# Block-sparse attention into a soft mixture of experts: the chunk selection packed two row blocks to a transpose

## The chip, the cores and the metric

One core of one Trainium2 chip runs the whole kernel in one launch. The metric is the device time of that launch in microseconds (us). The three runs before the change took 177.64, 177.72 and 176.17 us; their median is 177.64.

## The reference

Attention with a per-query choice of key chunks comes first: 4 batches, 8 heads, 768 positions, head size 64. Keys are grouped in 24 chunks of 32. For every query an upper bound of its score against each chunk is made from the chunk's elementwise minimum and maximum; the six causal chunks with the highest bound stay, all other keys are masked. A soft mixture of experts over 3072 tokens follows (512 features, 8 experts, 4 slots each).

```python
k_min, k_max = np.min(k_chunks, axis=3), np.max(k_chunks, axis=3)
ub = np.sum(np.maximum(q * k_min, q * k_max), axis=-1)          # per query and chunk
ub = np.where(causal, ub, -1000000000.0)
top_chunks = np.argsort(ub, axis=-1)[..., -top_k:]              # top_k = 6
scores = scale * np.matmul(q, k.transpose(0, 1, 3, 2))
mask = sel & (pos[:, None] >= pos[None, :])
attn = softmax(np.where(mask, scores, -1000000000.0))
x = np.matmul(attn, v)                                          # then tokens x features
logits = x @ phi                                                # (3072, 32)
slot_input = softmax(logits, axis=0).T @ x
slot_out = per_expert(relu(slot_input @ w1) @ w2)
return softmax(logits, axis=1) @ slot_out
```

## The kernel before

Heads are worked in pairs: 16 pairs, one per iteration `i` of the main loop (line 469), with 128 positions as a *row block* (six per pair, `NQT`). The two heads of a pair lie on partitions 0 to 63 and 64 to 127. The instruction order on each engine is written out by hand (`tc.manual_schedule()`), as a software pipeline: iteration `i` computes scores and exponentials of pair `i` (six groups `g`, `scores` and `expo`), the bounds and the selection of pair `i+1` (`ubound`, `select`, `ns_transposes`, `evac_ns`), loads, transposes and chunk minima and maxima of pair `i+2` (`transposes`, `evac_T`, `kmin`, `kmax`, `qsplit`), the product with V of pair `i-1` (`pv`), and the normalised output of pair `i-2`. After every fourth pair a batch is complete, and the `moe_*` steps of that batch (logits, running softmax, dispatch) are put into the iterations that follow: `moe_logits` at the ends of iterations 5, 9 and 13, `moe_max` to `moe_ct` in 6, 10 and 14. After the loop come the last batch, the experts and the output.

Who does what. TensorE (PE) does every product and transpose. ScalarE (ACT) does all exponentials (line 289) and copies the transposed k and q out of PSUM (line 193). VectorE (DVE) does minima and maxima, the top-8 search (line 242), the comparison (line 245), the copy of the transposed selection (line 261), normalisation and the rest of the copies. GpSimd (POOL) issues all input DMAs (lines 120, 127, 132) and masks the diagonal blocks (line 291). Each iteration asks for k and q of pair `i+4`, v of pair `i+2` and, in most iterations, 1 MB of expert weights, all on one DMA queue.

The selection goes through these tiles. `ub_ps` holds the bounds, `[128 queries, 6 row blocks, 2 heads x 24 chunks]`. `mx` takes the eight largest of each 24. `ns_t` (two static buffers) is a row of 64 columns per head and row block: in columns 0 to 23 a 1 where the chunk is *not* selected, in column 24 the largest bound (written by POOL, line 244), zeros beyond. Six PE transposes (line 253) turn it into `ns_ps`, with the heads on partitions 0 to 63 and 64 to 127, and DVE copies 768 columns to `nsT`. In `scores`, each group adds to the products of k and q, in the same PSUM tile, a second product of `smask` and `nsT`: `smask` has -1e9 in the rows of a chunk and -1 in row 24, so unselected keys sink and the largest bound is subtracted before the exponential. A group is up to 512 query columns of one or two key blocks:

```python
GROUPS = [[(0, 0, 512, 0)], [(1, 0, 512, 0)], [(2, 0, 512, 0)],
          [(4, 0, 256, 0), (0, 512, 256, 256)],
          [(3, 0, 384, 0), (1, 512, 128, 384)], [(5, 0, 128, 0)]]
```

The two score buffers (`p_sc`, `bufs=2`) alternate, so group `g+2` cannot start before the exponential of group `g` has read its buffer. The PSUM pool `p_tp` (two buffers) serves all transposes, bounds, logits and small products in turn.

Of the kernel before, what the change touches and what calls it, by code (L numbers as in the profile page):

```python
# [10 lines left out]
F32 = mybir.dt.float32  # L11
BF16 = mybir.dt.bfloat16
ALU = mybir.AluOpType
# [4 lines left out]
NEG = -1e9  # L18
CH = 32
NCHUNK = 24  # L20
NQT = 6
P = 128
S = 768
# [23 lines left out]
def kernel(  # L47
# [10 lines left out]
    nc = tc.nc  # L58
# [12 lines left out]
    static = ctx.enter_context(tc.tile_pool(name="static", bufs=1))  # L71
# [4 lines left out]
    p_tp = ctx.enter_context(tc.tile_pool(name="p_tp", bufs=2, space=PSUM))  # L76
    st = {}
# [7 lines left out]
    c_pad = static.tile([P, NQT, 4, CH], BF16, name="c_pad")  # L85
# [6 lines left out]
    identf = static.tile([P, P], F32, name="identf")  # L92
    ones_sq = static.tile([P, P], BF16, name="ones_sq")
    caus = static.tile([P, NQT, 2, NCHUNK], BF16, name="caus")
    qgrp = static.tile([P, 4, CH], BF16, name="qgrp")
    smask = static.tile([P, NQT, 4, CH], BF16, name="smask")
    schunk = static.tile([P, NCHUNK, 1], BF16, name="schunk")
    headsel = static.tile([P, 1, 2, 1], BF16, name="headsel")
    ns_t = [static.tile([P, NQT, 2, 64], BF16, name=f"ns_t{i}") for i in range(2)]

    small = ctx.enter_context(tc.tile_pool(name="small", bufs=1))
    xp = ctx.enter_context(tc.tile_pool(name="xp", bufs=2))
# [3 lines left out]
    tp2 = i_ctx.enter_context(tc.tile_pool(name="tp2", bufs=2, side="right"))  # L106
# [5 lines left out]
    def load_w(i):  # L112

        if i < E:
            src = moe_w1[i].rearrange("(a p x) f -> p a (x f)", p=P, x=2)
            dst = w_sb[i].rearrange("p (a f) -> p a f", a=NDG // 2)
        else:
            src = moe_w2[i - E].rearrange("(a p x) d -> p a (x d)", p=P, x=4)
            dst = w_sb[i].rearrange("p (a f) -> p a f", a=NFG // 4)
        nc.gpsimd.dma_start(out=dst, in_=src)  # L120

    def load(i, nm):

# [16 lines left out]
    make_identity(nc, ident)  # L140
    load(1, "k")
    load(1, "q")
    for t in (caus, qgrp, headsel, schunk, ns_t[0], ns_t[1], c_pad):
        nc.vector.memset(t, 0.0)
    nc.vector.memset(ones_sq, 1.0)
    for t in v_t:
# [1 line left out]
    for h in range(2):  # L148
# [10 lines left out]
    load(2, "k")  # L159
    load(2, "q")  # L160
    load_w(0)
    for h in range(2):
        sl = schunk[h * 64:(h + 1) * 64]
        nc.gpsimd.affine_select(
            out=sl, in_=sl, compare_op=ALU.not_equal, fill=NEG, base=0,
            pattern=[[-1, NCHUNK], [0, 1]], channel_multiplier=1,
        )
        nc.gpsimd.affine_select(
            out=sl, in_=sl, compare_op=ALU.not_equal, fill=-1.0, base=-NCHUNK,
            pattern=[[0, NCHUNK], [0, 1]], channel_multiplier=1,  # L170
        )
    load_v(0)
    load_v(1)
    nc.gpsimd.dma_start(out=phi_sb, in_=moe_phi.rearrange("(hg p) s -> p hg s", p=P))
# [45 lines left out]
        st["qpn", i] = t  # L220

    def ubound(i):
        ps = p_tp.tile([P, NQT, 2 * NCHUNK], F32, name="ub_ps", tag="tp")
        qpn, bd = st.pop(("qpn", i)), st.pop(("bd", i))
        for t in range(NQT):
            nc.tensor.matmul(
                ps[:, t, :], lhsT=qgrp.rearrange("p a b -> p (a b)"),
                rhs=caus[:, t].rearrange("p h c -> p (h c)"), start=True, stop=False,
            )
            for x in range(2):  # L230
                nc.tensor.matmul(  # L231
                    ps[:, t, :], lhsT=qpn[:, x, t * P:(t + 1) * P],
                    rhs=bd[:, x].rearrange("p h c -> p (h c)"),
                    start=False, stop=(x == 1),
                )
        st["ubps", i] = ps

    def select(i):
        ub = st.pop(("ubps", i)).rearrange("p t (h c) -> p (t h) c", h=2)
        mx = tpu.tile([P, NQT * 2, 8], F32, name="mx", tag="mx")  # L240
        for a in range(NQT * 2):
            nc.vector.max(mx[:, a, :], ub[:, a, :])  # L242
        ns = ns_t[i % 2].rearrange("p t h c -> p (t h) c")
        nc.gpsimd.tensor_copy(ns[:, :, NCHUNK:NCHUNK + 1], mx[:, :, 0:1])
        nc.vector.tensor_tensor(
            ns[:, :, :NCHUNK], ub,
            mx[:, :, TOPK - 1:TOPK].broadcast_to([P, NQT * 2, NCHUNK]), op=ALU.is_lt,
        )

    def ns_transposes(i):  # L250
        ps = p_tp.tile([P, NQT, P], BF16, name="ns_ps", tag="tp")
        for t in range(NQT):
            nc.tensor.matmul(  # L253
                ps[:, t, :], lhsT=ns_t[i % 2][:, t].rearrange("p h c -> p (h c)"),
                rhs=ident, is_transpose=True,
            )
        st["nsps", i] = ps

    def evac_ns(i):
        t = tp2.tile([P, S], BF16, name="nsT", tag="nsT")  # L260
        nc.vector.tensor_copy(t, st.pop(("nsps", i)).rearrange("p t c -> p (t c)"))  # L261
        st["nsT", i] = t

    def scores(i, g):
        ps = p_sc.tile([P, 2, 512], F32, name="sc_ps", tag="sc")
        kT, qT, nsT = st["kT", i], st["qT", i], st["nsT", i]
        for kg, q0, w, c in GROUPS[g]:
            qs = slice(kg * P + q0, kg * P + q0 + w)
            for h in range(2):
                r = slice(h * 64, (h + 1) * 64)  # L270
                nc.tensor.matmul(  # L271
                    ps[:, h, c:c + w], lhsT=kT[r, kg * P:(kg + 1) * P], rhs=qT[r, qs],
                    start=True, stop=False,
                )
            for h in range(2):
                r = slice(h * 64, (h + 1) * 64)
                nc.tensor.matmul(  # L277
                    ps[:, h, c:c + w], lhsT=smask[r, kg].rearrange("p a b -> p (a b)"),
                    rhs=nsT[r, qs], start=False, stop=True,
                )  # L280
        st["scps", i, g] = ps

    def expo(i, g):
# [185 lines left out]
    for i in range(-2, NPAIR):  # L469
# [64 lines left out]
        if have(i + 2):  # L534
            qsplit(i + 2)
        if i == -2:
            nc.scalar.copy(smask.rearrange("p t a x -> p (t a) x"), schunk.broadcast_to([P, NCHUNK, CH]))
        moe(moe_ct, i - 3)
        moe(moe_logits, i - 2)
        moe(moe_copy, i - 2)  # L540
# [33 lines left out]
    op = ctx.enter_context(tc.tile_pool(name="op", bufs=5))  # L574
# [3 lines left out]
    for g in range(2):  # L578
        sl = slice(g * 16, (g + 1) * 16)
# [5 lines left out]
    for g in range(2):  # L585
        sl = slice(g * 16, (g + 1) * 16)
# [121 lines left out]
```

## Time and profile before

| What | Value |
|---|---|
| Runs | 177.64, 177.72, 176.17 us |
| The profiled execution: its time, its span | 177.53 us, 175.8 us |
| PE busy (share of the span) | 139.1 us (79%) |
| DVE busy | 128.8 us (73%) |
| ACT busy | 120.0 us (68%) |
| POOL busy | 99.9 us (57%) |
| Bytes moved by DMA | 32.92 MB, mean 187 GB/s |

The span runs from the first to the last instruction of the program; 1.7 us of the execution lie around it. A busy share says how long an engine had something in work, not that it sets the pace: the 16 iterations, the first loads and the end after the loop have different limits, and the sections on them must be read one by one. Matmuls are pipelined and their ends are modelled, so a PE that is nearly always busy need not be at its limit. Times in the prediction are counted from the span's start.

### The profile page before, as it was taken

The numbers are of one execution on the slowest core, as the hardware profiler recorded it, in microseconds if no ns is written. First come the engines' busy times: TensorE is split into PE (matmuls) and PEld (weight loads), VectorE is DVE, ScalarE is ACT, GpSimd is POOL, SyncE is SP. The second block draws the span as 40 slices with busy tenths as digits, with TensorE's granted clock in tenths as the row PEclk, the third lists the DMA queues.
The fourth block names the chain that finished last, engine by engine and source line by source line (L and its number), as shares of the span: only waits on it lengthen the run. The fifth ranks groups of instructions, "written<-read, shape, count | busy, mean of one in ns | idle before, by whom it ended". The sixth has DMA issues, their size and how long they took to land.

```text
span 175.8 us, 5994 instructions
## 1 busy us (share of the span) xinstructions
PE 139.1 (79%) x2486; PEld 95.9 (55%) x2486; DVE 128.8 (73%) x429; ACT 120.0 (68%) x163; POOL 99.9 (57%) x194
## 2 busy tenths in 40 slices
PE   0449888999889889999988999999689569986500
PEld 0334556777567657766765776677467444532000
DVE  4456979999889998999998999999752650246530
ACT  2336798989789778988977698897667321156430
POOL 7995679869768557877775585759344600000000
PEclk9999999999999999999999999999999956999755
DMA  3999999999999999999999999199999993009995
GB/s 50 167 158 180 194 206 200 206 197 209 179 212 193 215 185 143 200 172 203 172 147 203 169 207 141 17 187 211 200 214 214 213 215 72 4 13 403 402 405 212
DMA packets 40460, 32.92 MB, mean 187 GB/s; under 512 B 26353, under 2 KB 34545, under 8 KB 40433
## 3 DMA queue, kind: packets, MB, share of 16 engines
q0 software_dynamic: 38416, 26.25, 101.8%
q1 hardware_dynamic: 2016, 6.29, 9.1%
q8 instruction: 19, 0.31, 0.7%
q14 instruction: 9, 0.07, 0.1%
HBM read 52.49 MB, written 6.29 MB: 334 GB/s over the span
## 4 chain that ended last, share of the span: by engine, by line
PE 36%; ACT 19%; DVE 13%; DMA 12%; POOL 11%; issue 5%; POOLq 0%; DVEq 0%; ACTq 0%
ACT e_sb L289 13%; DMA k_in<-in_k_dram 7%; PE sc_ps L271 6%; DMA out_dram<-o_sb 5%; PE at_ps L308 5%; PE sc_ps L277 4%; PE tr_ps L184 3%; PE h_ps L605 3%; DVE x_sb L321 3%; POOL e_sb L291 3%; POOL q_in L127 2%; PE ns_ps L253 2%; POOL k_in L127 2%; PE so_ps L640 2%; PE si_ps L427 2%
## 5 line engine op out<-in xcount | busy, mean ns | idle before, releaser
L289 ACT ACTIVATE e_sb<-sc_ps 128x1024 bf16<-128x1024 f32 x96 | 83.6, 936 | 10.9 <-PE sc_ps L277 9.9
L291 POOL TENSOR_SCALAR_AFFINE_SELECT e_sb<-e_sb 128x256 bf16<-128x256 bf16 x96 | 39.5, 423 | 32.7 <-ACT e_sb L289 32.0
L271 PE MATMUL sc_ps<-qT,kT 64*128 64x512 bf16 (+3 forms) x256 | 39.6, 310 | 6.6 <-ACT e_sb L289 6.3
L277 PE MATMUL sc_ps<-nsT,smask 64*128 64x512 bf16 (+3 forms) x256 | 36.8, 306 | 0.0
L308 PE MATMUL at_ps<-v_t,e_sb 128*128 128x65 bf16 x672 | 29.4, 194 | 1.2 <-DVE x_sb L321 1.1
L308 PEld LDWEIGHTS <-e_sb 128*128 128x128 bf16 x672 | 25.1, 98 | 3.4 <-DVE x_sb L321 1.6
L271 PEld LDWEIGHTS <-kT 64*128 64x128 bf16 x256 | 15.8, 94 | 16.8 <-issue 8.7
L242 DVE MAX8 mx<-ub_ps 128x8 f32<-128x24 f32 x192 | 18.8, 170 | 4.6 <-PE ub_ps L231 4.5
L202 DVE TENSOR_REDUCE mm<-kT 128x24 bf16<-128x768 bf16 x16 | 15.2, 949 | 4.0 <-ACT kT L193 4.0
L132 POOL DMA_DIRECT2D v_t<-in_v_dram x16 | 16.7, 1042 | 1.9 <-PE ns_ps L253 1.2
L193 ACT COPY kT<-tr_ps 128x768 bf16<-128x768 bf16 x16 | 12.8, 803 | 6.5 <-PE tr_ps L184 6.5
L321 DVE TENSOR_TENSOR x_sb<-at_ps,inv 128x768 bf16<-128x768 f32 (+2 forms) x17 | 15.5, 910 | 0.6
L277 PEld LDWEIGHTS <-smask 64*128 64x128 bf16 x256 | 13.1, 95 | 4.4 <-issue 0.3
L208 DVE TENSOR_REDUCE mm<-kT 128x24 bf16<-128x768 bf16 x16 | 15.1, 942 | 0.0
L193 ACT COPY qT<-tr_ps 128x768 bf16<-128x768 bf16 x16 | 13.2, 825 | 2.7 <-PE tr_ps L184 2.7
L184 PE MATMUL tr_ps<-ident,k_in 128*64 128x128 bf16 x192 | 9.2, 237 | 6.6 <-DMA k_in<-in_k_dram 5.5
L670 DVE TENSOR_SCALAR o_sb<-o_ps,cinv 128x512 f32<-128x512 f32 x12 | 8.6, 748 | 7.2 <-PE o_ps L668 4.1
L231 PE MATMUL ub_ps<-bd,qpn 128*128 128x48 bf16 x192 | 10.4, 187 | 2.8 <-DVE qpn L218 2.5
L127 POOL DMA_DIRECT2D k_in<-in_k_dram x16 | 11.7, 729 | 1.3 <-POOLq L692 0.8
L261 DVE COPY nsT<-ns_ps 128x768 bf16<-128x768 bf16 x16 | 8.9, 556 | 4.0 <-PE ns_ps L253 3.5
L672 ACT ACTIVATE o_sb<-o_ps,cinv 128x512 f32<-128x512 f32 x12 | 7.8, 688 | 5.7 <-DMA out_dram<-o_sb 3.8
L127 POOL DMA_DIRECT2D q_in<-in_q_dram x16 | 11.5, 721 | 0.0
(95 smaller groups left out, 213.2 us busy)
## 6 DMA issues: line engine op xcount, KB each, us to landing
w_sb<-in_moe_w_dram POOLq DMA_DIRECT2D x16, 1024.0 KB, 12.9
out_dram<-o_sb SPq DMA_DIRECT2D x10, 512.0 KB, 5.5
k_in<-in_k_dram POOLq DMA_DIRECT2D x16, 192.0 KB, 7.9
q_in<-in_q_dram POOLq DMA_DIRECT2D x16, 192.0 KB, 8.1
v_t<-in_v_dram POOLq DMA_DIRECT2D x16, 192.0 KB, 9.3
out_dram<-o_sb SPq DMA_DIRECT2D x4, 256.0 KB, 3.4
phi_sb<-in_moe_phi_dram POOLq DMA_DIRECT2D x1, 32.0 KB, 9.6
```

The costliest lines, as they stand in the source:

```text
L127: nc.gpsimd.dma_start(out=t, in_=src.rearrange("h (p g) d -> p h (g d)", p=P))
L132: nc.gpsimd.dma_start(out=v_t[i % NV][:, :, :, :D], in_=v[b, 2 * j:2 * j + 2].rearrange("h (g p) d -> p h g d", p=P),)
L193: nc.scalar.copy(t.rearrange("d (p g) -> d p g", g=NQT), st.pop((nm + "ps", i)).rearrange("d g p -> d p g"),)
L202: nc.vector.tensor_reduce(mm[:, 0, 0, :], kT, axis=AX.X, op=ALU.min)
L208: nc.vector.tensor_reduce(mm[:, 1, 0, :], kT, axis=AX.X, op=ALU.max)
L242: nc.vector.max(mx[:, a, :], ub[:, a, :])
L271: nc.tensor.matmul(ps[:, h, c:c + w], lhsT=kT[r, kg * P:(kg + 1) * P], rhs=qT[r, qs], start=True, stop=False,)
L277: nc.tensor.matmul(ps[:, h, c:c + w], lhsT=smask[r, kg].rearrange("p a b -> p (a b)"), rhs=nsT[r, qs], start=False, stop=True,)
L289: nc.scalar.activation(e[:, :, :w], st.pop(("scps", i, g))[:, :, :w], func=ACT.Exp, scale=scale)
L291: nc.gpsimd.affine_select(out=e[:, :, :P], in_=e[:, :, :P], compare_op=ALU.is_ge, fill=0.0, base=0, pattern=[[0, 2], [1, P]], channel_mult ...
L308: nc.tensor.matmul(o, lhsT=st["e", i, g][:, h, c:c + P], rhs=v_t[i % NV][:, h, kg, :], start=(kg == 0), stop=(kg == t),)
L321: nc.vector.tensor_tensor(st["x", b][:, t0:t1, 2 * j:2 * j + 2, :].rearrange("p t h d -> p h t d"), at[:, :, :, :D], inv.broadcast_to([P, ...
```

## The change

The selection row shrinks from 64 to 32 columns per head and row block, and two neighbouring row blocks (`2j` and `2j+1`, the last index `x` of the bounds tile) share one transpose: `ns_t` is `[128, 3, 2 heads, 2, 32]`. Three transposes per pair replace six, and the copy to `nsT` has 384 columns instead of 768. After the transpose a head's 64 partitions hold the even row block in their first 32 rows and the odd one in the other 32, in the same columns. `smask` therefore exists twice, once with its rows filled in the first half of a head's partitions and once in the second; the other half is zero. A mask product over several row blocks becomes two, one for the blocks of the first one's parity and one for the others, each writing every second 128-column block of the PSUM tile (`2*m-1` blocks in steps of two); a single block needs one, as before. Per pair and head this makes 14 mask products out of 8. The top-8 search of row block `t` reads only the first `4t+4` chunks (at least 8) instead of 24. In the setup, two selects over 96 columns replace four over 24, one small DVE addition joins the heads' halves, and the ACT copy that spreads `schunk` to `smask` has 1536 columns instead of 768. Order of work on every engine, and everything not named here, stays.

```diff
-    smask = static.tile([P, NQT, 4, CH], BF16, name="smask")
-    schunk = static.tile([P, NCHUNK, 1], BF16, name="schunk")
+    smask = static.tile([P, 2, NQT, 4, CH], BF16, name="smask")
+    NJ = NQT // 2
+    squad = static.tile([P, 2, 2, NCHUNK], BF16, name="squad")
+    schunk = static.tile([P, 2, NCHUNK, 1], BF16, name="schunk")
...
-    ns_t = [static.tile([P, NQT, 2, 64], BF16, name=f"ns_t{i}") for i in range(2)]
+    ns_t = [static.tile([P, NJ, 2, 2, CH], BF16, name=f"ns_t{i}") for i in range(2)]
...
-    for h in range(2):
-        sl = schunk[h * 64:(h + 1) * 64]
-        nc.gpsimd.affine_select(out=sl, ...)
-        nc.gpsimd.affine_select(out=sl, ...)
+    nc.gpsimd.affine_select(out=squad, ...)
+    nc.gpsimd.affine_select(out=squad, ...)
...
     def ubound(i):
-        ps = p_tp.tile([P, NQT, 2 * NCHUNK], F32, name="ub_ps", tag="tp")
+        ps = p_tp.tile([P, NJ, 2, 2, NCHUNK], F32, name="ub_ps", tag="tp")
         for t in range(NQT):
+            o = ps[:, t // 2, :, t % 2, :]
...
     def select(i):
         for a in range(NQT * 2):
-            nc.vector.max(mx[:, a, :], ub[:, a, :])
+            t = 2 * (a // 4) + a % 2
+            nc.vector.max(mx[:, a, :], ub[:, a, :max(8, 4 * t + 4)])
...
     def ns_transposes(i):
-        for t in range(NQT):
+        for t in range(NJ):
...
     def evac_ns(i):
-        t = tp2.tile([P, S], BF16, name="nsT", tag="nsT")
+        t = tp2.tile([P, NJ * P], BF16, name="nsT", tag="nsT")
...
     def scores(i, g):
-            for h in range(2):
-                r = slice(h * 64, (h + 1) * 64)
-                nc.tensor.matmul(
-                    ps[:, h, c:c + w], lhsT=smask[r, kg].rearrange("p a b -> p (a b)"),
-                    rhs=nsT[r, qs], start=False, stop=True,
-                )
+            t0, n = kg + q0 // P, w // P
+            for x in range(min(2, n)):
+                f = t0 + x
+                m = (n - x + 1) // 2
+                k0 = c // P + f - t0
+                for h in range(2):
+                    r = slice(h * 64, (h + 1) * 64)
+                    nc.tensor.matmul(
+                        ps[:, h].rearrange("p (k y) -> p k y", y=P)[:, k0:k0 + 2 * m - 1:2, :],
+                        lhsT=smask[r, f % 2, kg].rearrange("p a b -> p (a b)"),
+                        rhs=nsT[r, f // 2 * P:(f // 2 + m) * P].rearrange("p (k y) -> p k y", y=P),
+                        start=False, stop=(x == min(2, n) - 1),
+                    )
...
         if i == -2:
-            nc.scalar.copy(smask.rearrange("p t a x -> p (t a) x"), schunk.broadcast_to([P, NCHUNK, CH]))
+            nc.vector.tensor_tensor(schunk[:, :, :, 0], squad[:, :, 0, :], squad[:, :, 1, :], op=ALU.add)
+            nc.scalar.copy(
+                smask.rearrange("p o t a x -> p (o t a) x"),
+                schunk.rearrange("p o c x -> p (o c) x").broadcast_to([P, 2 * NCHUNK, CH]),
+            )
```

More of the change, by code (lines that the diff above doesn't have):

```diff
@@ L142 @@
     load(1, "q")
-    for t in (caus, qgrp, headsel, schunk, ns_t[0], ns_t[1], c_pad):
+    for t in (caus, qgrp, headsel, squad, ns_t[0], ns_t[1], c_pad):
         nc.vector.memset(t, 0.0)
@@ L161 @@
     load_w(0)
-    for h in range(2):
-        sl = schunk[h * 64:(h + 1) * 64]
-        nc.gpsimd.affine_select(
-            out=sl, in_=sl, compare_op=ALU.not_equal, fill=NEG, base=0,
-            pattern=[[-1, NCHUNK], [0, 1]], channel_multiplier=1,
-        )
[L168 to L171, printed above, removed]
+    nc.gpsimd.affine_select(
+        out=squad, in_=squad, compare_op=ALU.not_equal, fill=NEG, base=0,
+        pattern=[[-CH, 2], [-64, 2], [-1, NCHUNK]], channel_multiplier=1,
+    )
+    nc.gpsimd.affine_select(
+        out=squad, in_=squad, compare_op=ALU.not_equal, fill=-1.0, base=-NCHUNK,
+        pattern=[[-CH, 2], [-64, 2], [0, NCHUNK]], channel_multiplier=1,
+    )
     load_v(0)
@@ L222, in ubound @@
     def ubound(i):
-        ps = p_tp.tile([P, NQT, 2 * NCHUNK], F32, name="ub_ps", tag="tp")
+        ps = p_tp.tile([P, NJ, 2, 2, NCHUNK], F32, name="ub_ps", tag="tp")
         qpn, bd = st.pop(("qpn", i)), st.pop(("bd", i))
         for t in range(NQT):
+            o = ps[:, t // 2, :, t % 2, :]
             nc.tensor.matmul(
-                ps[:, t, :], lhsT=qgrp.rearrange("p a b -> p (a b)"),
-                rhs=caus[:, t].rearrange("p h c -> p (h c)"), start=True, stop=False,
+                o, lhsT=qgrp.rearrange("p a b -> p (a b)"), rhs=caus[:, t], start=True, stop=False,
             )
@@ L231, in ubound @@
                 nc.tensor.matmul(
-                    ps[:, t, :], lhsT=qpn[:, x, t * P:(t + 1) * P],
-                    rhs=bd[:, x].rearrange("p h c -> p (h c)"),
+                    o, lhsT=qpn[:, x, t * P:(t + 1) * P],
+                    rhs=bd[:, x],
                     start=False, stop=(x == 1),
@@ L238, in select @@
     def select(i):
-        ub = st.pop(("ubps", i)).rearrange("p t (h c) -> p (t h) c", h=2)
+        ub = st.pop(("ubps", i)).rearrange("p j h x c -> p (j h x) c")
         mx = tpu.tile([P, NQT * 2, 8], F32, name="mx", tag="mx")
         for a in range(NQT * 2):
-            nc.vector.max(mx[:, a, :], ub[:, a, :])
-        ns = ns_t[i % 2].rearrange("p t h c -> p (t h) c")
+            t = 2 * (a // 4) + a % 2
+            nc.vector.max(mx[:, a, :], ub[:, a, :max(8, 4 * t + 4)])
+        ns = ns_t[i % 2].rearrange("p j h x c -> p (j h x) c")
         nc.gpsimd.tensor_copy(ns[:, :, NCHUNK:NCHUNK + 1], mx[:, :, 0:1])
@@ L250, in ns_transposes @@
     def ns_transposes(i):
-        ps = p_tp.tile([P, NQT, P], BF16, name="ns_ps", tag="tp")
-        for t in range(NQT):
+        ps = p_tp.tile([P, NJ, P], BF16, name="ns_ps", tag="tp")
+        for t in range(NJ):
             nc.tensor.matmul(
-                ps[:, t, :], lhsT=ns_t[i % 2][:, t].rearrange("p h c -> p (h c)"),
+                ps[:, t, :], lhsT=ns_t[i % 2][:, t].rearrange("p h x c -> p (h x c)"),
                 rhs=ident, is_transpose=True,
@@ L274, in scores @@
                 )
-            for h in range(2):
-                r = slice(h * 64, (h + 1) * 64)
-                nc.tensor.matmul(
-                    ps[:, h, c:c + w], lhsT=smask[r, kg].rearrange("p a b -> p (a b)"),
-                    rhs=nsT[r, qs], start=False, stop=True,
-                )
+            t0, n = kg + q0 // P, w // P
[10 more added lines that the diff above has]
+                        start=False, stop=(x == min(2, n) - 1),
+                    )
         st["scps", i, g] = ps
@@ L536 @@
         if i == -2:
-            nc.scalar.copy(smask.rearrange("p t a x -> p (t a) x"), schunk.broadcast_to([P, NCHUNK, CH]))
+            nc.vector.tensor_tensor(schunk[:, :, :, 0], squad[:, :, 0, :], squad[:, :, 1, :], op=ALU.add)
+            nc.scalar.copy(
+                smask.rearrange("p o t a x -> p (o t a) x"),
+                schunk.rearrange("p o c x -> p (o c) x").broadcast_to([P, 2 * NCHUNK, CH]),
+            )
         moe(moe_ct, i - 3)
```

## The prediction

> **What bounds the kernel now.** I read the page first, for the engines and the DMA row, then ACT's and PE's timeline over one ordinary iteration, the chain of work that ended last, and the DMA landings.
>
> ```profile
> PE 139.1 (79%) x2486; PEld 95.9 (55%) x2486; DVE 128.8 (73%) x429; ACT 120.0 (68%) x163; POOL 99.9 (57%) x194
> PEclk9999999999999999999999999999999956999755
> DMA  3999999999999999999999999199999993009995
> ```
>
> Three engines are close together, so the totals do not name the bound. The DMA row is full from the second slice (4.4 us) to the 25th (110 us), and the TensorE clock drops once behind the loop, near 141 us. The timeline of an ordinary iteration (start, length, engine, line, idle time before and who ended it):
>
> ```profile
> 75.61 1.94 ACT L289 ACTIVATE e_sb<-sc_ps 128x1024 bf16<-128x1024 f32 x2 [0.48 <-PE sc_ps L277]
> 77.44 0.81 ACT L193 COPY kT<-tr_ps 128x768 bf16<-128x768 bf16 x1
> 78.12 1.97 ACT L289 ACTIVATE e_sb<-sc_ps 128x1024 bf16<-128x1024 f32 x2
> 79.94 0.84 ACT L193 COPY qT<-tr_ps 128x768 bf16<-128x768 bf16 x1
> 80.62 1.37 ACT L289 ACTIVATE e_sb<-sc_ps 128x1024 bf16<-128x1024 f32 x2
> 81.76 0.39 PE L271 MATMUL sc_ps<-qT,kT 64*128 64x512 bf16 x2 [0.19 <-ACT e_sb L289]
> 82.47 1.94 ACT L289 ACTIVATE e_sb<-sc_ps 128x1024 bf16<-128x1024 f32 x2 [0.48 <-PE sc_ps L277]
> ```
>
> ACT has no idle time but 0.48 us per iteration: the first scores of the next pair wait for the fifth exponential to free a buffer (81.76), and ACT waits for them (82.47). That loop, 82.47 - 75.61 = 6.86 us, comes back in iterations 1, 3, 7, 8, 11 and 12, so six of sixteen are bound by ACT. The others are longer: 5, 9 and 13 (7.2 to 7.4 us) end with `moe_logits` on PE, 6, 10 and 14 (9.2 to 10.3) carry the rest of a batch's expert routing, and 4 waits for a load. Two pieces of the chain (start, length, what) show it, the load first:
>
> ```profile
> 33.22 12.54 DMA k_in<-in_k_dram
> 45.80 0.53 PE tr_ps L184 x12
> ...
> 118.63 0.44 PE ns_ps L253 x6
> 119.07 0.70 PE at_ps L308 x22
> 119.77 0.61 PE lg_ps L350 x24
> ...
> 122.60 1.09 DVE mx L242 x12
> ...
> 127.34 0.44 PE ns_ps L253 x6
> ```
>
> So the changed operations are on the path at routing iterations only, and everything ahead of 45.8 us meets a DMA that has been full since 4.4 us.
>
> **The change, part by part.** *Selection transposes.* Six take 0.44 to 0.46 us in the chain, 0.075 each; three fewer save 0.22 us per pair.
>
> ```profile
> L242 DVE MAX8 mx<-ub_ps 128x8 f32<-128x24 f32 x192 | 18.8, 170 | 4.6 <-PE ub_ps L231 4.5
> L261 DVE COPY nsT<-ns_ps 128x768 bf16<-128x768 bf16 x16 | 8.9, 556 | 4.0 <-PE ns_ps L253 3.5
> L341 DVE COPY xT_sb<-xT_ps 128x768 bf16<-128x768 bf16 x14 | 7.7, 549 | 2.2 <-PE xT_ps L330 2.1
> L341 DVE COPY xT_sb<-xT_ps 128x256 bf16<-128x256 bf16 x1 | 0.3, 292 | 0.5 <-PE xT_ps L330 0.5
> L277 PE MATMUL sc_ps<-nsT,smask 64*128 64x256 bf16 x64 | 7.8, 269 | 0.0
> L277 PEld LDWEIGHTS <-smask 64*128 64x128 bf16 x256 | 13.1, 95 | 4.4 <-issue 0.3
> ```
>
> These are groups by shape (count, busy us, mean ns of one, idle before). *The copy* of 384 columns: line 341 costs 549 ns for 768 columns and 292 for 256, 0.50 ns each, so 0.36 us against 0.56, a saving of 0.20. *The maxima*: twelve take 1.15 us. A pair's lengths fall from 12 x 24 to 2 x (8+8+12+16+20+24), 112 elements fewer. A float element from PSUM costs 1.03 ns (line 321: 957 ns for 768, 693 for 512), so up to 0.115 us; if a search is a fixed cost, nothing. I take 0.11, because 89 ns from start to start leave room for 24 elements.
>
> *The mask products* rise from 16 to 28 per pair, 192 in all; with 48 transposes gone PE has 144 matmuls more. The streamed columns stay the same, and the two heads run side by side. In the timeline a 512-column pair of heads takes 0.21 to 0.23 us from start to start (77.38, 77.61, 77.82), a 256-column pair 0.11 (77.82, 77.93, 78.04, 78.15) and a 128-column pair 0.05 (79.84, 79.89). Two halves are as long as the whole, each with its own weight load, so I cost the twelve at nothing. What hides the loads is the matmul before them; uncovered, each extra pair costs 95 ns (the line 277 load), which is the upper end. A gain is excluded, since no column disappears. *Bounds* (lines 226, 231): same count and columns, written in two pieces of 24; nothing, and if their 26 ns spacing doubled, 18 x 26 = 0.47 us per pair.
>
> A rule speaks against this part. The Trainium skill, "TensorE: Matmul & The Clock Gate", section "Back-to-back issue gap", gives about 81 ns per matmul at N=128 and 131 at N=512 for streams of weight load and matmul. By it a head pair's 512 columns would cost 262 ns whole and, between its two figures, some 390 in halves; the 0.22 us measured here is less than either. The estimate by that page is 0.13 x 6 = 0.78 us of PE more per pair, about 0.55 net of the transposes.
>
> *Setup.* Four POOL selects (0.34 to 0.39 us each) become two over 96 columns (128x128 takes 0.33, 4x288 takes 0.51, so 0.66 to 1.0 together); I take 0.7, and POOL is 0.7 us earlier. Its selection cast at 12.71 gates the first transposes (13.00), which at the first, slower clock take 0.82 us and become 0.41. Pair 0's scores thus come about 1.1 us earlier. The spread copy on ACT grows from 0.83 us to about 1.4 (exponentials: 430 ns for 256 columns, 1037 for 1024, so 0.79 ns each) and ends near 11.3, where the next copy starts (11.29); the new DVE addition (0.2 us by the 0.18 and 0.29 us of lines 401 and 210) lies in the 0.92 us before 10.50. The memsets lie before the first load lands. No DMA moves in any queue.
>
> **Where it reaches the path.** Ahead of 45.8 us: 1.1 us saved, all given back. The k of pair 6 was issued at 33.22 behind a queue that is never empty; landings follow at one transfer's length, and the first issue (1.31) does not move. PE waited 0.65 us for it and will wait some 1.2 longer there or, in part, one iteration earlier (k of pair 5 landed at 37.64, 0.6 us ahead of need). Without that cover the 1.1 us would count.
>
> The ACT-bound iterations: nothing, the loop holds no changed operation but the mask product. The routing iterations:
> - 5 to 6: scores(6,0) stand behind transposes, `pv` and logits on PE: -0.22. At the end of 6 the PE chain from 65.90 to 68.12 starts with the transposes, and the fifth exponential allows 0.18 of their 0.22. Together 0.40.
> - 9 to 10: DVE saves 0.42 before the logits' copy (89.29), but logits end at 89.20 and move by 0.22 to 0.25: 0.25. Inside 10 the fifth exponential waits for `c_pad`, behind DVE work that holds no changed operation: nothing.
> - 13 to 14: -0.22 ahead of the logits, -0.11 in the maxima (in the chain there), -0.22 in the transposes at 127.34: 0.55.
>
> Sum 0.40 + 0.25 + 0.55 = 1.20 us. The profiled execution took 177.53 (span 175.8 and 1.7 around it), which gives 176.33; the median of the runs lies 0.11 above it, so 176.4.
>
> **The rivals.** *The early gain gets through.* If k of pair 6 lands earlier with the compute, the 1.1 us add to it: 176.4 - 1.1 = 175.3. For it: DMA rates of 158 to 206 GB/s in the slices up to 40 us, so the queue is not at one fixed speed. Against it: landings 9 to 15 us after issue all that time.
>
> *The cold clock takes half.* Per the windows view PE's clock is granted at 0.73 from 138 to 144.7 and 0.63 to 149; the expert products at 144.75 run at half pace until about 148. If work comes 1.2 us earlier and the clock does not, 0.6 us are lost again: 177.0. The lowest run (176.17) may have met a shorter stretch; that stretch can move the time by about 1 us either way.
>
> *The split products show their loads.* At 95 ns per extra pair, six per iteration, PE gains 0.57 - 0.22 = 0.35 us of work. An ordinary iteration has 0.22 of PE idle (6.64 busy of 6.86), so 7, 8, 11 and 12 grow by 0.13 each (0.5), 5, 9 and 13, where PE is full (7.32 of 7.37), by 0.3 each (0.9), and 6, 10 and 14 by some 0.1 for the first scores (0.3): 177.5 + 1.7 = 179.2, slower. It decides from 0.22/6 = 37 ns per pair, where PE's work no longer falls. For it: PE is the fullest engine. Against it: the 256- and 128-column rows.
>
> **How the numbers follow.** Forecast 176.4 (its own range 175.4 to 177.2) 0.46; early gain through 0.24; cold clock 0.10; loads exposed 0.20. One per cent is 1.8 us, about what a measurement of this kernel can tell from no change: the three runs spread by 1.5. Faster by that means under 175.9: the second case and a third of the first, 0.40. Slower means over 179.4; the last case lies around there, and its upper end (both loads of a pair in turn, 190 ns) is far beyond, so it is counted there whole: 0.20. The rest is 0.40. The range 174.4 to 178.6 takes in the early gain with a luckier clock and, upwards, a lost gain with an unluckier one, and leaves out the exposed loads.
>
> **What would show it.** Right: ordinary iterations stay at 6.85; the wait of `tr_ps` for `k_in` near 45.8 grows past 1 us with its end where it was; the 256-column mask pairs start 0.11 apart; the `nsT` copy takes 0.36 us; three transposes take 0.23. Wrong: k of pair 6 landing well before 45; a period of 6.95 or more in iterations 7, 8, 11, 12; mask pairs over 0.15 apart; the end after the loop differing by more than 1 us.

## The result and the profile after

The changed kernel takes 175.69 us (median of 18 runs, 174.44 to 177.01) against 176.94 (18 runs, 175.96 to 177.92) for the kernel before on the same chips. The ratio is 0.9923, its 95% interval [0.9901, 0.9946]: 1.25 us by the medians, faster by less than one per cent. The profiled execution took 176.33 us with a span of 174.6. The forecast was 176.4 from a saving of 1.20. The time itself came out 0.7 lower, because the median of the kernel before fell from 177.64 (3 runs) to 176.94 (18 runs). The size of the saving came out; the places did not all, and that the sum fits is in part luck, as told below.

The page of the changed kernel, engines, TensorE clock and DMA row:

```profile
PE 136.6 (78%) x2629; PEld 100.3 (57%) x2630; DVE 124.8 (71%) x430; ACT 120.5 (69%) x163; POOL 98.8 (57%) x192
PEclk9999999999999999999999999999999956999855
DMA  3999999999999999999999999199999994009995
```

PE runs 143 matmuls more and is busy 2.5 us less, DVE 4.0 us less, and the DMA row is as full as before. The next table divides the two profiled executions at the start of each pair's first exponential (timeline of ACT, line 289 before, 297 after), then at the first expert product, the first output product and the end of the last computing instruction (169.50 and 168.24 us; the 6.3 to 6.4 us behind it, in which the output is still being written, are left out).

| Stretch | Before | After | Change | Forecast |
|---|---|---|---|---|
| start to pair 0 | 15.60 | 14.82 | -0.78 | -1.1 |
| iterations 0 to 4 | 36.46 | 36.46 | 0.00 | +1.1 |
| 5 and 6 | 16.70 | 17.17 | +0.47 | -0.40 |
| 7 and 8 | 13.71 | 13.71 | 0.00 | 0 |
| 9 and 10 | 17.64 | 17.26 | -0.38 | -0.25 |
| 11 and 12 | 13.71 | 13.71 | 0.00 | 0 |
| 13 and 14 | 16.39 | 15.95 | -0.44 | -0.55 |
| pair 15 to the experts | 14.47 | 14.23 | -0.24 | 0 |
| experts to first output product | 11.26 | 11.63 | +0.37 | 0 |
| output | 13.56 | 13.30 | -0.26 | 0 |

An ordinary iteration after, on ACT, with the PE line that ends its wait (start, length, engine, line, operation, idle before and who ended it):

```profile
75.30 1.94 ACT L297 ACTIVATE e_sb<-sc_ps 128x1024 bf16<-128x1024 f32 x2 [0.48 <-PE sc_ps L283]
...
80.31 1.37 ACT L297 ACTIVATE e_sb<-sc_ps 128x1024 bf16<-128x1024 f32 x2
...
81.45 0.39 PE L272 MATMUL sc_ps<-qT,kT 64*128 64x512 bf16 x2 [0.36 <-ACT e_sb L297]
...
82.16 1.02 ACT L297 ACTIVATE e_sb<-sc_ps 128x1024 bf16<-128x1024 f32 x1 [0.48 <-PE sc_ps L283]
```

The same 6.86 us, with the same 0.48 us of idle ACT. PE now waits 0.36 us for the fifth exponential where it waited 0.19: its saving became idle time. The mask products on PE in that iteration:

```profile
77.07 0.39 PE L272 MATMUL sc_ps<-qT,kT 64*128 64x512 bf16 x2
77.30 0.38 PE L283 MATMUL sc_ps<-nsT,smask 64*128 64x256 bf16 x4
77.51 0.27 PE L272 MATMUL sc_ps<-qT,kT 64*128 64x256 bf16 x2
77.62 0.28 PE L283 MATMUL sc_ps<-nsT,smask 64*128 64x128 bf16 x4
77.73 0.27 PE L272 MATMUL sc_ps<-qT,kT 64*128 64x256 bf16 x2
```

Four products of 256 columns (two head pairs) take 77.30 to 77.51, 0.21 us, the time of one whole pair of 512 before; four of 128 take 0.11. The extra weight loads do not show. The groups by shape (count, busy us, mean ns of one, idle before) give the sizes of the other terms:

```profile
L243 DVE MAX8 mx<-ub_ps 128x8 f32<-128x8 f32 x64 | 6.3, 158 | 6.1 <-PE ub_ps L231 5.0 <-POOL e_sb L299 0.9 <-issue 0.2
L262 DVE COPY nsT<-ns_ps 128x384 bf16<-128x384 bf16 x16 | 5.6, 352 | 2.0 <-PE ns_ps L254 1.9
L243 DVE MAX8 mx<-ub_ps 128x8 f32<-128x24 f32 x32 | 5.4, 169 | 0.0
L164 POOL TENSOR_SCALAR_AFFINE_SELECT squad<-squad 128x96 bf16<-128x96 bf16 x1 | 0.3, 317 | 0.0
L168 POOL TENSOR_SCALAR_AFFINE_SELECT squad<-squad 128x96 bf16<-128x96 bf16 x1 | 0.3, 285 | 0.1
```

The chain of work around the k of pair 6 and the end of iteration 5 (start, length, what):

```profile
32.00 13.26 DMA k_in<-in_k_dram
45.26 0.04 issue
45.31 0.53 PE tr_ps L184 x12
...
56.09 0.27 PE ns_ps L254 x3
56.36 0.70 PE at_ps L316 x22
57.07 0.54 PE lg_ps L358 x22
57.61 0.56 issue
58.16 0.21 PE lg_ps L358 x2
```

The chain still comes out of that load. Three transposes take 0.27 us where six took 0.44. And PE stops for 0.56 us in the middle of the logits with nothing in the trace that releases it ("issue"): that is what turned iterations 5 and 6 from a gain into a loss here.

### The profile page after: what moved, and what is told of

The parts are those of the page before. It is cut to its first block, busy times and chain, and to the rows that moved or that the text cites. A ratio compares the mean times of both kernels' runs of the same rounds, so it can differ in the third digit from the quotient of the medians.

```text
span 174.6 us, 6281 instructions
## 1 busy us (share of the span) xinstructions
PE 136.6 (78%) x2629; PEld 100.3 (57%) x2630; DVE 124.8 (71%) x430; ACT 120.5 (69%) x163; POOL 98.8 (57%) x192
## 4 chain that ended last, share of the span: by engine, by line
PE 36%; ACT 21%; DMA 15%; DVE 14%; POOL 6%; issue 4%; SPq 0%; ACTq 0%; POOLq 0%; DVEq 0%
ACT e_sb L297 14%; DMA k_in<-in_k_dram 10%; PE sc_ps L272 6%; DMA out_dram<-o_sb 5%; PE tr_ps L184 4%; PE sc_ps L283 4%; PE at_ps L316 4%; PE h_ps L617 3%; ACT kT L193 3%; POOL e_sb L299 3%; PE ub_ps L231 2%; DVE x_sb L329 2%; PE so_ps L652 2%; PE ub_ps L227 2%; DVE mm L202 2%
## 5 line engine op out<-in xcount | busy, mean ns | idle before, releaser
L283 PE MATMUL sc_ps<-nsT,smask 64*128 64x256 bf16 (+1 forms) x448 | 37.1, 245 | 0.0
L283 PEld LDWEIGHTS <-smask 64*128 64x128 bf16 x448 | 23.0, 95 | 7.3 <-issue 0.5
L243 DVE MAX8 mx<-ub_ps 128x8 f32<-128x8 f32 (+2 forms) x192 | 17.0, 161 | 6.1 <-PE ub_ps L231 5.0
L329 DVE TENSOR_TENSOR x_sb<-at_ps,inv 128x768 bf16<-128x768 f32 (+2 forms) x17 | 15.5, 911 | 0.6
L122 POOL DMA_DIRECT2D w_sb<-in_moe_w_dram x16 | 11.4, 714 | 0.0
```

The lines of the kernel that those rows point to most:

```text
L243: nc.vector.max(mx[:, a, :], ub[:, a, :max(8, 4 * t + 4)])
L283: nc.tensor.matmul(ps[:, h].rearrange("p (k y) -> p k y", y=P)[:, k0:k0 + 2 * m - 1:2, :], lhsT=smask[r, f % 2, kg].rearrange("p a b -> p ...
L329: nc.vector.tensor_tensor(st["x", b][:, t0:t1, 2 * j:2 * j + 2, :].rearrange("p t h d -> p h t d"), at[:, :, :, :D], inv.broadcast_to([P, ...
```

## Experiments

The theory: compute saved ahead of pair 6 turns into a longer wait for its k, ordinary iterations gain nothing, and the transposes, the copy and the maxima pay in the routing iterations 5, 6, 9, 13 and 14 alone. The main rival: the early saving gets through and the routing share is small. A ratio below is to the kernel before, with its 95% interval.

**The changed kernel again**, unaltered.

> The changed kernel unaltered, for a second profile. Theory (the saving is made at the routing iterations 5, 6, 9, 10, 13, 14; all that is saved ahead of 45.8 us is lost to the load of k for pair 6): ratio to the kernel before 0.992 to 0.994; PE waits 1.0 to 1.4 us for that load; iterations 1 to 3, 7, 8, 11, 12 last 6.85 us. In the first profile of the changed kernel the load landed at 45.26 instead of 45.76, and PE paused 0.56 us inside the logits of iteration 5 (57.61) with nothing released at its end. If both belong to the program they come again within 0.1 us; if they are chance, the landing lies anywhere from 45 to 46 and the pause is gone, and iteration 5 takes 7.1 to 7.2 us instead of 7.73. Rival (the early gain gets through): the landing is again 0.5 us or more ahead of 45.76.

0.9925 [0.9898, 0.9952], 175.80 us. In this profile the k of pair 6 landed at 44.88 and PE waited 0.65 us for it, the pause in iteration 5 was 0.24 us instead of 0.56, and everything from iteration 6 to 14 repeats within 0.04 us. So the landing, the length of that wait (1.21 us in the first profile) and the length of the pause are no fixed part of the kernel.

**Only the split of the mask products**, in the kernel before (rows of 64 columns kept):

```diff
-                nc.tensor.matmul(ps[:, h, c:c + w], lhsT=smask[r, kg]..., rhs=nsT[r, qs], ...)
+            for x in range(min(2, n)):
+                m = (n - x + 1) // 2
...
+                    nc.tensor.matmul(ps...[:, k0:k0 + 2 * m - 1:2, :], lhsT=smask[r, kg]...,
+                                     rhs=nsT...[:, b0 + x:b0 + x + 2 * m - 1:2, :], ...)
```

> The kernel before with nothing but its mask products split as in the change (one product over even and one over odd row blocks, 28 instead of 16 per pair; same weights for both halves, 64-column selection, six transposes, full maxima). Theory (split products cost nothing): ratio to the kernel before 0.999 to 1.002, ordinary iterations at 6.85 to 6.87 us, 256-column pairs of heads 0.11 us from start to start. Rival (weight loads exposed at 0.095 us per extra pair of products): ordinary iterations 6.95 us or more, total 2 to 4 us longer, ratio 1.01 to 1.02.

1.0007 [0.9977, 1.0037]. Ordinary iterations 6.85 us, the 256-column pairs 0.11 us apart. The rival of exposed loads (2 to 4 us slower in this kernel, by the expectation) is out.

**Each of the three transposes issued twice**, in the changed kernel:

```diff
-            nc.tensor.matmul(ps[:, t, :], lhsT=ns_t[i % 2][:, t]..., rhs=ident, is_transpose=True)
+            for _ in range(2):
+                nc.tensor.matmul(ps[:, t, :], lhsT=ns_t[i % 2][:, t]..., rhs=ident, is_transpose=True)
```

> The changed kernel with each of its three selection transposes issued twice (same operands, same output), so PE does six per pair as before, and all else stays as changed. Theory (the transposes are what counts, 0.22 us at each of the ends of iterations 5, 9, 13, and in 6 and 14): 0.9 to 1.1 us of the 1.25 are given back, ratio to the kernel before 0.997 to 0.999; e.g. the first exponential of pair 14 moves 0.4 to 0.7 us later than in the changed kernel, measured from that of pair 5. Rival (the gain is the shorter copy on VectorE): under 0.3 us given back, ratio 0.992 to 0.994. Rival (the early gain): at most 0.3 us given back.

0.9925 [0.9902, 0.9949]: by its time, nothing was lost. By its profile, the stretches that the transposes gate are longer than in the changed kernel: iterations 13 and 14 take 7.47 + 8.80 against 7.30 + 8.65 us, 6 takes 9.51 against 9.44. But the count of PE instructions has moved, and with it the pause: iteration 5 has none (7.19 us, against 7.42 and 7.73 in the two profiles of the changed kernel), iteration 9 has one of 0.50. With intervals of 0.4 us to each side and such pauses, this run does not decide.

**Maxima over all 24 chunks**, in the changed kernel:

```diff
-            nc.vector.max(mx[:, a, :], ub[:, a, :max(8, 4 * t + 4)])
+            nc.vector.max(mx[:, a, :], ub[:, a, :])
```

> The changed kernel with the top-8 search over all 24 chunks again. Theory: only iteration 14 has the searches in its chain, so 0.1 us are given back: ratio to the kernel before 0.992 to 0.995, the twelve searches take 1.15 us instead of about 1.03, and iteration 14 grows by 0.1 us. Rival (VectorE is close to the bound everywhere, so 0.11 us count in all 16 iterations): ratio 1.00 to 1.003.

0.9897 [0.9855, 0.9938], lower than the changed kernel itself, with an interval that holds it. In the profile iterations 13 and 14 are 0.10 us longer, the size of the term; the time cannot show it.

**The weight load moved**, in both kernels. If the wait for k of pair 6 hides the early saving, taking the backlog away must let it out. One of the 1 MB weight loads ahead of that k goes from iteration 0 to iteration 11:

```diff
-    for i in (2, 5, 8, 11):
+    for i in (0, 2, 5, 8):     # iterations without a weight load
```

> The kernel before, with the 1 MB weight load of iteration 0 issued in iteration 11 instead (both counts of the weight plan, nothing else), so that some 4.8 us of transfer no longer stand in the DMA queue ahead of the loads of pairs 4, 5 and 6. Theory (the wait for k of pair 6 is a queue wait and swallows what is saved ahead of it): the k loads of pairs 5 and 6 land 4 to 5 us earlier, no wait for them is left, 0.4 to 0.9 us saved in all: ratio to the kernel before 0.995 to 0.998. Rival (the early stage is bound by compute and the wait only a remainder): ratio 0.999 to 1.001, iteration 4 as long as before.

> The changed kernel with the same move of one weight load from iteration 0 to iteration 11. Theory: the 1.2 us that it waited for k of pair 6 come free, so it gains 0.7 to 1.2 us on the changed kernel: ratio to the kernel before 0.985 to 0.988, and the distance to the kernel before with the same plan grows to 1.8 to 2.2 us, since the start's 1.0 us then counts. The first exponential of pair 5 comes at about 50.0 us. Rival (what the start saves is lost in another wait): ratio 0.991 to 0.993.

The kernel before: 1.0007 [0.9981, 1.0032]. The changed kernel: 0.9872 [0.9830, 0.9915], 174.33 us, the fastest version here. By the two ratios the change is worth 1.35% or 2.4 us with this plan, against 0.77% without; the intervals of the two runs leave the 1.35 uncertain by about 0.5 to each side. In the profiles pair 15 starts 2.85 us earlier than in the kernel before with the same plan, but 0.51 of this lies in iteration 0. Its length goes with the moment from which the trace shows TensorE at full clock: in the profiles of the given order (but for the one with the copy twice) from 7.24 us with 15.5 to 8.08 with 18.8, and here 7.44 with 16.6 against 7.95 with 18.4. That moment differs between executions of one kernel, 17.6 and 18.3 in the two profiles of the changed one. The rest is 0.84 of the start, 0.46 in iterations 2 and 4, and 1.07 in 5, 6, 9, 10, 13 and 14. The waits view (us in total, times, longest), the changed kernel first, then with the moved load:

```profile
PE tr_ps L184 <- DMA k_in<-in_k_dram: 6.1, 2, 4.9
```

```profile
PE tr_ps L184 <- DMA k_in<-in_k_dram: 4.9, 1, 4.9
```

The 4.9 us are the first load of the program; the second wait, 1.21 us, is gone. The k of pair 6 lands at 39.74 in place of 45.26, iteration 4 falls from 8.08 to 6.85 us, and iteration 5 takes 7.02, without a pause. In the kernel before, iteration 4 falls too (7.81 to 7.09) and pair 15 starts 0.59 us earlier in the profile, but the times show none of it, with 0.45 us of interval to each side: the forecast of 0.995 to 0.998 was missed. The wait there was the short one (0.65 us).

**A start made later on purpose.** The second select of the setup runs three times, in the changed kernel and in the one with the moved load:

```diff
+    nc.gpsimd.affine_select(out=squad, in_=squad, ...)     # the same as the one before it
+    nc.gpsimd.affine_select(out=squad, in_=squad, ...)
```

> The changed kernel with the second setup select on POOL done three times instead of once (same result), so that the first selection cast, and with it pair 0, comes about 0.7 us later. Theory (what happens ahead of 45 us is covered by the wait for k of pair 6): the first exponentials of pairs 0 to 4 come 0.5 to 0.8 us later, that of pair 5 stays 6.0 us behind the landing of k of pair 6, and the time stays: ratio to the kernel before 0.991 to 0.994. Rival (the early gain gets through): 0.7 us longer than the changed kernel, ratio 0.996 to 0.997.

> The same later start in the changed kernel with the weight load moved from iteration 0 to 11. Theory: no load is waited for, so the 0.7 us (0.5 to 0.8) count: ratio to the kernel before 0.990 to 0.992 against 0.987 without the later start. Rival: as without it, 0.986 to 0.988.

Pair 0 starts only 0.35 us later in both. With the old plan (0.9937 [0.9906, 0.9968]) that is swallowed: k of pair 6 lands at 45.08, PE waits 0.42 us instead of 1.21, and pair 5 starts at 51.09, not later than 51.28. With the moved load (0.9900 [0.9863, 0.9937]) pair 5 starts at 50.02 against 49.67: all 0.35 come through. By the times alone the two runs with the moved load cannot be told apart (0.9900 and 0.9872, with intervals that overlap). In the profile pair 15 starts 1.44 us later, and what the start does not explain of it is a pause in the logits of iteration 5 (timeline):

```profile
57.31 0.20 PE L366 MATMUL lg_ps<-phi_sb,xT_sb 128*128 128x32 bf16 x2 [0.96 <-issue]
```

**The transposes twice, with the moved load**, to have the question of six transposes without the wait:

> The changed kernel with the weight load moved and each of the three selection transposes issued twice (same output). Theory (PE's three transposes are the larger part of the gain): iterations 5, 9 and 13 grow by 0.17 us each, 6 by 0.07 and 14 by 0.15, as in the run with six transposes and the old load plan, and the first stretch up to pair 5 by 0.3 to 0.6 us since it counts now: 1.0 to 1.3 us in all, ratio to the kernel before 0.992 to 0.995 against 0.987. Rival (the transposes are covered, as the time of that earlier run with 0.9925 suggests): under 0.4 us, ratio 0.987 to 0.989.

0.9940 [0.9909, 0.9971] against 0.9872: 0.68% or 1.2 us. In the profile pair 15 starts 1.54 us later: the routing iterations 5, 6, 9, 10, 13 and 14 give 0.17 + 0.06 + 0.17 + 0.06 + 0.16 + 0.19 = 0.81, iterations 7 and 8 0.21 each by a pause of PE, and iteration 2 another 0.20. That one is no pause: both operations that split q on DVE run into DMA issues of POOL there and take 0.91 and 0.81 us, the normalisation behind them comes late, and PE's product with V waits for it. Iteration 2 takes 7.05 to 7.14 us in all five profiles in the given order where both operations are long, the kernel before among them, and 6.85 in the others. The start was 0.33 later and iteration 0 0.19 shorter. So the transposes are worth about 0.8 us in the routing iterations and 0.3 at the start, and the pauses and meetings that they shift can weigh nearly as much.

**The copy of the selection twice, with the moved load:**

```diff
-        nc.vector.tensor_copy(t, st.pop(("nsps", i)).rearrange("p t c -> p (t c)"))
+        for _ in range(2):
+            nc.vector.tensor_copy(t, st["nsps", i].rearrange("p t c -> p (t c)"))
```

> The changed kernel with the weight load moved and the copy of the transposed selection done twice on VectorE (0.72 us together, 0.16 more than the one copy before the change; same result). Theory (the copy is covered by other work except at the start, where it stands once in the chain): 0.3 to 0.5 us longer in the first stretch, nothing in ordinary iterations, at most 0.1 us in each of 5, 9 and 13: ratio to the kernel before 0.988 to 0.991. Rival (VectorE is the bound of the iterations, so each 0.36 us counts): ordinary iterations over 6.95 us, 4 us or more in all, ratio over 1.00.

0.9972 [0.9941, 1.0004] against 0.9872, more than the 0.988 to 0.991 expected, while ordinary iterations stay at 6.85 us, against the rival. In the profile 1.24 us of it stand in iteration 1, where the granted clock was 0.5 from 22.23 to 25.65 us, and belong to that execution. Pair 0 starts at 14.66 against 14.81, and iteration 0 takes 0.51 more; whether that is the copy, as expected there, one profile cannot tell. Iterations 5, 9 and 13 stay (7.02, 7.02, 7.30), as expected; 6 and 10 do not, with 9.70 against 9.45 and 11.18 against 10.24 us. The timeline of DVE and POOL ahead of iteration 10, and PE inside it:

```profile
87.24 1.02 POOL L134 DMA_DIRECT2D v_t<-in_v_dram  x1 [0.60 <-PE ns_ps L254]
87.50 0.93 DVE L218 TENSOR_SCALAR qpn<-qT 128x768 bf16<-128x768 bf16 x1
88.26 0.70 POOL L122 DMA_DIRECT2D w_sb<-in_moe_w_dram  x1
88.34 0.80 DVE L219 TENSOR_SCALAR qpn<-qT 128x768 bf16<-128x768 bf16 x1
...
98.53 0.49 PE L450 MATMUL cT_ps<-ident,c_pad 128*128 128x128 bf16 x6 [0.41 <-DVE nsT L263]
```

The expectation left out that a DVE operation of 0.35 us can take 0.8 to 0.9 when it starts while POOL issues a DMA. The second copy moves both halves of the split into the next issues. Counted from the start of iteration 10, DVE's copy of the logits behind them starts 0.97 us later than with the moved load alone, and the iteration keeps 0.94 of it to its end. The wait in the last line is for a PSUM buffer that the copy has to release (0.41 us); it adds nothing to the next pair's start, since the delay is there in full before it.

**The fifth and sixth groups exchanged** (`scores` and `expo` of group 5 ahead of 4), in both kernels, to take ACT's 0.48 us of idle time away:

```diff
-            scores(i, 4)
-            expo(i, 4)
             scores(i, 5)
             expo(i, 5)
+            scores(i, 4)
+            expo(i, 4)
```

> The kernel before with the small last group of scores (128 columns) computed ahead of the fifth instead of behind it, so that the next pair's first scores wait for the short exponential and are ready when the long one ends. Theory (ordinary iterations are bound by ACT and this one buffer; PE has 0.22 us and VectorE 0.2 to 0.4 us to spare): ACT's 0.48 us of idle time goes, but PE and VectorE stop the iteration at 6.6 to 6.7 us: four such iterations count (7, 8, 11, 12), 0.6 to 1.0 us in all, ratio to the kernel before 0.994 to 0.997. Rival (another engine already sets the 6.85 us): 6.85 us as before, ratio 0.999 to 1.001.

> The changed kernel with the same swap of the last two groups. Theory (the change took 0.22 us per pair off PE and about 0.3 us off VectorE, which lies idle in ordinary iterations as long as ACT's loop sets them): iterations 7, 8, 11 and 12 fall to 6.40 to 6.50 us, 1.4 to 1.8 us saved on the changed kernel, twice what the swap saves on the kernel before; ratio to the kernel before 0.982 to 0.986. Rival (PE has no such slack, because the split mask products cost it what the transposes save): 6.6 to 6.7 us as in the kernel before with the swap, ratio 0.987 to 0.990.

The kernel before: 1.0237 [1.0207, 1.0267], 181.03 us. The changed one: 1.0007 [0.9977, 1.0038], 176.85. The order is worse in both. I had counted PE's busy time and ACT's idle time, not the order on PE. In the exchanged kernel before, iteration 9 (one with logits) on PE and ACT ends so:

```profile
88.88 0.34 PE L271 MATMUL sc_ps<-qT,kT 64*128 64x384 bf16 x2 [0.29 <-ACT e_sb L289]
...
89.43 0.51 PE L253 MATMUL ns_ps<-ident,ns_t 128*128 128x128 bf16 x6
89.77 0.87 PE L308 MATMUL at_ps<-v_t,e_sb 128*128 128x65 bf16 x22
90.48 0.75 PE L350 MATMUL lg_ps<-phi_sb,xT_sb 128*128 128x32 bf16 x24
91.16 0.39 PE L271 MATMUL sc_ps<-qT,kT 64*128 64x512 bf16 x2
...
91.87 1.02 ACT L289 ACTIVATE e_sb<-sc_ps 128x1024 bf16<-128x1024 f32 x1 [1.14 <-PE sc_ps L277]
```

The group that waits for a free score buffer now stands ahead of the selection's transposes, the product with V, the logits and the next pair's first scores, all in one queue, and ACT idles 1.14 us behind them. Ordinary iterations became 6.92 to 7.08 us, and in the changed kernel 6.76 to 7.15. With PE this close to the pace the change is worth 2.3% (4.2 us by the medians), three times what it is worth in the given order. In the two profiles the routing iterations 5, 6, 9, 10, 13 and 14 give 2.2 us of it, 1 to 3, 7, 8, 11 and 12 together 0.5; the rest lies at the two ends and in iteration 0 (1.60, with a later full clock in the slower one, 22.47 against 16.50 us), less 1.45 that the changed kernel lost in iteration 4, where it waited 1.84 us for k of pair 6. So the edit's worth depends on what bounds the iteration, the ordinary ones included.

## Why the prediction was right, and where only its sum was

*The wait for k of pair 6*: right in kind, too large in size. The wait ended on the landing and grew from 0.65 to 1.21 us in the first two profiles (waits view, us in total, times, longest; the rest is the first load of the program):

```profile
PE tr_ps L184 <- DMA k_in<-in_k_dram: 5.5, 2, 4.9
```

But its length goes with the landing: 0.65 and 0.41 us in the kernel before and the split kernel, 1.21, 0.65, 1.13 and 1.26 in the two profiles of the changed kernel, with the transposes twice and with the full maxima: some 0.5 more on average, where 1.2 more was forecast. A later start cost nothing with the old load plan and its full 0.35 us with the moved one; without the wait the change is worth about 2.4 us.

*The early saving*, forecast 1.1, was 0.78. The two selects cost 0.60 as against 0.7, and the selection cast comes 0.73 us earlier (11.98 instead of 12.71). But the first transposes come only 0.45 earlier, because the cast no longer gates them. In the kernel before, then in the changed one:

```profile
8.64 0.52 DVE L218 TENSOR_SCALAR qpn<-qT 128x768 bf16<-128x768 bf16 x1
13.00 0.82 PE L253 MATMUL ns_ps<-ident,ns_t 128*128 128x128 bf16 x6 [1.75 <-POOL ns_t L244]
```

```profile
8.67 0.91 DVE L218 TENSOR_SCALAR qpn<-qT 128x768 bf16<-128x768 bf16 x1
12.55 0.48 PE L254 MATMUL ns_ps<-ident,ns_t 128*128 128x128 bf16 x3 [0.95 <-ACT kT L193]
```

POOL's issue of v now starts at 8.38, before the split of q and not behind it, and the split takes 0.91 us. The bounds, the transposes of k behind them and ACT's copy of k (11.64 instead of 11.29) come later for it, and that copy is what the transposes now wait for. With two more selects (0.57 us) the issue starts at 9.23, the split takes 0.35, and so the start moved by 0.35 only.

*"All given back"*: not literally. Pair 5 starts 0.78 us earlier in the profile. Of this 0.50 is the landing itself (45.26 against 45.76) and 0.29 a shorter way from landing to exponential (6.30 us before, 6.31 in the split kernel; 6.01 in five profiles of the new selection). Landings do not follow the compute: 45.76, 45.46 and 44.55 in kernels of the old selection, 45.26, 44.88, 45.13, 45.57, 45.08 and 45.17 in those of the new, means 45.26 and 45.18. With three landings against six that spread by 1.2 and 0.7 us, the rival "early gain gets through" has no support as a mechanism, but a few tenths of it cannot be excluded; I take the 0.50 as this execution's. The 0.29 is real and was not forecast: in the kernel before and the split one ACT starts the second exponential after that load (47.75 in the first) 0.40 us after its products end, with nothing in the trace between; in those five it starts 0.10 after them. That iteration 2 is 0.23 shorter, by the DMA issues told at the run with the transposes twice and the moved load, was not forecast either; it stands ahead of that wait.

*Ordinary iterations and split products at nothing*: right, by the table, the split kernel and the spacing of the pairs. PE busy in such an iteration fell from 6.64 to 6.49 us (the one shown), and nothing came of it.

*Iterations 5 and 6, -0.40*: wrong in size. Without a pause 5 goes from 7.19 to 7.02 (-0.17, forecast -0.22) and 6 from 9.51 to 9.44 (-0.07, forecast -0.18). The mis-sized terms are the three transposes, 0.17 us saved instead of 0.22, and the share that the fifth exponential "allows" at the end of 6. A pause of 0.24 to 0.56 us on PE, not in the sum, then cost more than that in four of five profiles with the old plan.

*9 and 10, -0.25*: measured -0.38. In the kernel before, the DVE operation on q met the DMA issue of v, as it no longer does after (timelines of DVE and POOL, before and after). They met in all three kernels with the old selection and this order, where 9 and 10 take 17.64 to 17.66 us together, and again with the transposes twice and the moved load, where they take 17.49 against 17.27. So 0.22 of the 0.38 are the transposes with the meeting that they bring; the full maxima change nothing here (17.26), and the rest falls to the copy by subtraction alone.

```profile
88.02 1.19 POOL L132 DMA_DIRECT2D v_t<-in_v_dram  x1 [0.60 <-PE ns_ps L253]
88.23 0.35 DVE L218 TENSOR_SCALAR qpn<-qT 128x768 bf16<-128x768 bf16 x1
88.50 0.87 DVE L219 TENSOR_SCALAR qpn<-qT 128x768 bf16<-128x768 bf16 x1
```

```profile
87.57 0.35 DVE L218 TENSOR_SCALAR qpn<-qT 128x768 bf16<-128x768 bf16 x1
87.71 1.11 POOL L134 DMA_DIRECT2D v_t<-in_v_dram  x1 [0.60 <-PE ns_ps L254]
87.84 0.35 DVE L219 TENSOR_SCALAR qpn<-qT 128x768 bf16<-128x768 bf16 x1
```

*13 and 14, -0.55*: -0.44, split otherwise: 13 is 0.11 longer (ACT starts the first exponential of pair 14 some 0.38 us after its products end, in every profile of the new layout, and 0.10 after them in the others), 14 0.56 shorter. Transposes and maxima take their parts in it, by the runs that put them back: 0.32 (0.17 + 0.15) and 0.10 us.

*The copy*: 0.352 us, forecast 0.36. *The maxima*: 158 ns for 8 elements, 169 for 24, twelve in 1.03 us instead of 1.15, as forecast.

*The end*: forecast unchanged. The experts' stretch is 0.37 us longer in the profile, the cold clock's rival in part: half clock for 6.8 us in both, but earlier against the work. The second profile of the changed kernel has 3.4 us of it and a stretch of 10.66, so this term belongs to the execution. The output is at least 0.20 shorter in all kernels with the new selection than in the others (13.51 to 13.57); its cause was not found. The 0.24 between pair 15 and the experts belong to the execution: 14.24 and 14.47 us come in kernels of both selections.

So the routing iterations give 1.06 without the pause (0.24, 0.38 and 0.44) where 1.20 was forecast, and that part of the mechanism held. In the profiled pair the pause takes 0.71 of it, and 0.78 that were forecast as lost come through ahead of pair 5. Neither was in the sum, and that the two nearly cancel is luck.

## What to carry to other kernels

Price an edit by iteration: first find which iterations its engine ends, then which wait ends the stretch before a late load, and read the same operation's spacing on the trace instead of its count. A saving ahead of a full load queue shows only after something is taken out of that queue, so try the move of a load together with the edit: here the move alone gave nothing that the times show, the edit alone 0.8%, both 1.3%. Where a gain is a few tenths of a microsecond, compare stretches of several profiles and not times, and look for pauses that moved with the instruction count.

## What the runs showed of the hardware

*PE pauses at fixed places in its instruction stream.* The pauses marked "issue" came, counted in matmuls and weight loads, before instruction 1719 (the changed kernel and three of its kind, 0.24 to 0.56 us, and 0.96 with the moved load and late start), 2996 (transposes twice), 3251 (the split kernel) and 2230, 2486 and 4273 (transposes twice with the moved load). All these numbers lie within 7 of each other modulo 256. The Trainium skill, "Runtime: NRT & Kernel Launch", section "Instruction fetch mechanics", says that an engine's instructions are refilled in 16 KiB blocks of 256 by DMA, and that this is mostly hidden; the traces have 19 and 20 transfers of 16 KB on a queue named "instruction". The times of these transfers fit: with the n-th of them put to the n-th block of 256, each of the pauses ends 1.23 to 1.53 us after the transfer of its block has landed, and in none of the fourteen profiles is the place 183 of a block reached sooner than 1.23 us after it. That fits a PE that stops where it comes too early for its refill. No run took the refills away, and whether the full DMA engines make them late was not tested.

*A DVE operation and a DMA issue of POOL.* Each half of the split of q mostly takes 0.34 to 0.35 us, and up to 0.93 where it starts during a DMA issue, ending about 0.16 us after that issue. In iteration 5 after, the timeline reads:

```profile
56.30 1.02 POOL L134 DMA_DIRECT2D v_t<-in_v_dram  x1
56.42 0.35 DVE L262 COPY nsT<-ns_ps 128x384 bf16<-128x384 bf16 x1
56.69 0.79 DVE L218 TENSOR_SCALAR qpn<-qT 128x768 bf16<-128x768 bf16 x1
57.41 0.34 DVE L219 TENSOR_SCALAR qpn<-qT 128x768 bf16<-128x768 bf16 x1
```

From the start of the copy to the end of the split it is 1.33 us here, and was 1.18 before with the longer copy (57.36 to 58.54): the copy's 0.20 us were given back at once. The Trainium skill, "SBUF — State Buffer", section "Who interferes with whom", has GpSimd share a pair of ports with DVE's two-port modes, and whoever comes first holds them for its whole instruction; the rows agree that the later DVE operation pays. But in the issue at 87.71 above, the operations at 87.57 and 87.84 took 0.35 us both. What decides in the issues of v is how far the issue has come. Over all fourteen profiles, the 35 operations that started in its first 0.23 us took 0.35 to 0.43; the 108 that started 0.26 to 0.6 us into it all lasted until 0.15 to 0.21 us after its end, 0.64 to 0.93 us in all. In the shorter issues of the weights this line does not hold (0.80 us from 0.08 into one).
